# One fixed instruction list kept through the first GEMM half: conversion, stores, steps and the list's order changed together

## The chip, the cores and the metric

The kernel runs on one core of a Trainium2 chip. The metric is the device time in microseconds (us) from launch to the end of the program. Each engine (TensorE = PE, VectorE = DVE, ScalarE = ACT, GpSimd = POOL, SyncE = SP, which issues most of the DMAs) runs its own instructions in the order in which they were placed, and engines wait for each other through semaphores. The order on each engine is fixed when the program is built.

## The reference

Eight batches of Nystrom attention with 32 landmarks per head feed a dense MLP (W_in, squared ReLU, W_out), whose output goes through a top-1 mixture of eight experts.

```
attention, per batch (8 heads, 576 tokens, 64 wide), landmarks = means over 18 tokens:
    A = softmax(q k_lm^T);  Bm = softmax(q_lm k_lm^T);  C = softmax(q_lm k^T)
    Z = Bm^T / (norm1(Bm) * norminf(Bm) + 1e-6);  6 times: Z = 2 Z - Z Bm Z
    out = A Z C v
MLP:      x = relu(x @ w_in)**2 @ w_out          (512 -> 2048 -> 512)
experts:  e = argmax(x @ w_gate); out = gate * sigmoid(x @ w_og)[e] * (relu(x @ w1[e]) @ w2[e])
```

## The kernel before

**GEMM halves.** The MLP is done per batch b and half c of its tokens (288 columns), in `gemm(b)`. Each of the 16 steps f makes `hp` (6 matmuls of the attention factors `ab` and `gb`), squares it into `gh` + `gl` (high and low part: ACT makes `r` and `gh`, DVE makes `g` and `gl`; in half (0, 0) `g` is on DVE, later on ACT), and two steps later `second` adds 12 matmuls into the four `acc` banks, with W_out as `hi` (ACT) and `lo` (DVE). `ab` is the softmaxed A, transposed and split; `gb` is W_in folded into the batch's 64-wide factor (`chunk`: matmuls `two<-wi,wt`, then `split_g` on ACT and DVE), four chunks of four steps each. So the matmuls of step f need `ab`, `gb`, and two steps later `hi` and `lo`.

**Conversion.** W_in and W_out arrive as 64-bit floats in 32 pieces of 512 KB (`raw`). `convert` is a generator: each turn fetches the piece three ahead, scales one piece (`m` by a cast on POOL, ACT or DVE, and `r` on ACT) and adds the two integer halves of the piece before (`bits`, POOL, written to `wf` or `w`). `cv()` in the prologue and `convert_on(f)` in half (0, 0) turn it, `CONV` turns per step f; `split_out(f)` turns it further when W_out piece f isn't there yet. Converted W_in pieces go back to DRAM (`win`) through a list of held stores, which `release(n)` empties.

**Steps of later batches.** The attention of batch b + 1 (`unit`) is a generator too; `point()` takes `RATES[b, c]` steps at each of its places in the GEMM (58 places in half (0, 0), 64 in others), so that the steps run beside the matmuls. Its parts named below: `sums` and `landmarks` (`lm`), `scores_a` and `scores_c` (both `two<-x,lm` on PE), `softmax_b` (many small DVE instructions on `mb`, `bt`, `bc`), `inverse`, `weights` (`wz`, `wt`), `softmax_a` (`aa`: subtract and multiply on POOL, Exp on ACT, sums on DVE), `transposed_a` (`at`). After `gemm`'s last step of a batch, `finish` writes logits (`pl`) and `route` picks experts (`pt`, `pc`).

**The list of tied operations.** While `self.strict` is true, `in_lane` ties every instruction to the one written before it on its engine, so the engine's order is the order of the code. With `strict` False new instructions follow the last tied one but are free among themselves: a scheduler with its own timing estimate chooses their order. With `strict` None nothing is tied.

```
        if self.strict is not None and hasattr(op, "ins"):
            if name in self.lanes:
                self.follow(op, self.lanes[name])
            if self.strict:
                self.lanes[name] = op
```

Before, the tied list covers the prologue and ends with the last line of `first_g`. In `gemm(0)` at c = 1, f = 0, conversion is finished, the held stores are released and `strict` becomes None.

Of the kernel before, what the change touches and what calls it, by code (L numbers as in the profile page):

```python
# [9 lines left out]
F32 = mybir.dt.float32  # L10
# [7 lines left out]
ALU = mybir.AluOpType  # L18
# [5 lines left out]
LM = 32  # L24
# [16 lines left out]
CONV_BUFS = 3  # L41


CONV = 2.0
SUMS_AT = {3: ("k", 0), 5: ("k", 1), 7: ("q", 0)}
OUT_AHEAD = 3
FIRST_G = (6, 10)
# [1 line left out]
URGENT = 2000  # L49
G_FIRST = 2  # L50

RATES = {(0, 0): 0.2, (0, 1): 0.65}
RATE = 0.4

PACE = 20
# [65 lines left out]
class Kernel:  # L121
# [60 lines left out]
    def convert(self, jobs):  # L182

        nc, pool = self.nc, self.cv
        W = CONV_W
        pieces = [(j, c) for j in range(len(jobs)) for c in range(0, 512, W)]
        st, to = {}, {}
        RB = CONV_AHEAD

        tops = [pool.tile([128, W], I32, tag=f"cm{i}", name="m") for i in range(CONV_BUFS)]
        for m in tops:
            nc.gpsimd.memset(m, 0)  # L200

        def fetch(i):

            j, c = pieces[i]
            raw = pool.tile([128, 2 * W], I32, tag="raw", name="raw", bufs=RB)
            self.raws[i] = nc.sync.dma_start(
                out=raw.bitcast(U16)[:, 0:4 * W - 1], in_=jobs[j][0][:, c:c + W].bitcast(U16)[:, 1:4 * W]
            )
            st[i] = raw

        def scale(i):

            raw, m = st[i], tops[i % CONV_BUFS]
            r = pool.tile([128, W], I32, tag="cr", name="r", bufs=CONV_BUFS)
            top = m.bitcast(F16).rearrange("p (n t) -> p n t", t=2)[:, :, 1]
            high = raw.bitcast(BF16).rearrange("p (n t) -> p n t", t=4)[:, :, 2]
            ops = []
            if self.strict and i > 4 and i % 2:
                ops.append(nc.scalar.activation(out=top, in_=high, func=ACTF.Copy))
            elif self.strict or i % 2:  # L220
                ops.append(nc.gpsimd.tensor_copy(out=top, in_=high))
            else:
                ops.append(nc.vector.tensor_copy(out=top, in_=high))
            ops.append(nc.scalar.activation(
                out=r, in_=raw.rearrange("p (n t) -> p n t", t=2)[:, :, 0].bitcast(U32), func=ACTF.Copy,
                scale=2.0 ** -13,
            ))
            if self.last_h is not None:
                for op in ops:
                    self.follow(op, self.last_h)  # L230
            st[i] = m, r

        def bits(i):
            (j, c), (m, r) = pieces[i], st.pop(i)
            if c == 0:
                to[j] = jobs[j][1]()
            self.halves(to[j][:, c:c + W].bitcast(I32), m, r, ALU.add)

        n = len(pieces)
        for i in range(min(RB - 1, n)):  # L240
            fetch(i)
        yield STEP
        per = 512 // W
        for i in range(n + 4):
            if i + RB - 1 < n:
                fetch(i + RB - 1)
            if i < n:
                scale(i)
            if 0 <= i - 1 < n:
                bits(i - 1)  # L250
            if i >= 2 and (i - 2) % per == per - 1 and i - 2 < n:
                j = (i - 2) // per
                jobs[j][2](to.pop(j))
            yield STEP
# [246 lines left out]
    def sums(self, u, nm, hg):  # L501

        if nm + "s" not in u:
            u[nm + "s"] = self.sm.tile([128, 2, 2, D], F32, tag=f"{nm}s", name="sums", bufs=1)
        s, t = u[nm + "s"][:, hg], self.qk[nm, u["b"], hg]
        if not u["pe"]:
            t = t.rearrange("p s d -> p (s d)")
            x = self.sm.tile([128, SEG // 2 * D], F32, tag="st", name="st", bufs=1)
            add = lambda out, in0, in1: self.nc.gpsimd.tensor_tensor(out=out, in0=in0, in1=in1, op=ALU.add)
            n = SEG * D // 4  # L510
            for c in range(0, 2 * n, n):
                self.paced(add(x[:, c:c + n], t[:, c:c + n], t[:, 2 * n + c:3 * n + c]))
            for w in (256, 128, 64):
                add(x[:, 0:w], x[:, 0:w], x[:, w:2 * w])
            twice = [128, 2, D]
            add(s, x[:, 0:D].unsqueeze(1).to_broadcast(twice), x[:, 512:576].unsqueeze(1).to_broadcast(twice))
            return
        for d in range(0, D, D // 2):
            ds = slice(d, d + D // 2)
            total = self.nc.vector.tensor_reduce(  # L520
                out=s[:, 0, ds], in_=t[:, :, ds].rearrange("p s d -> p d s"), axis=AX.X, op=ALU.add
            )
            if self.last_h is not None:
                self.follow(total, self.last_h)
# [102 lines left out]
    def exp_a(self, u, hg):  # L627

        nc = self.nc
        ma = u["ma"][:, :, hg]  # L630
        af = u["aa"][:, hg].rearrange("p (n l) -> p n l", l=LM)
        wide = [128, NB, LM]
        nc.vector.tensor_reduce(out=ma[:, 0], in_=af, axis=AX.X, op=ALU.max)
        yield
        nc.vector.tensor_tensor(
            out=af, in0=af, in1=ma[:, 0].unsqueeze(2).to_broadcast(wide), op=ALU.subtract
        )
        nc.scalar.activation(out=af, in_=af, func=ACTF.Exp, scale=SCALE / SEG)
        yield
        nc.vector.tensor_reduce(out=ma[:, 1], in_=af, axis=AX.X, op=ALU.add)  # L640
        nc.vector.tensor_scalar(out=ma[:, 1], in0=ma[:, 1], scalar1=1e-9, scalar2=None, op0=ALU.add)
        nc.vector.reciprocal(out=ma[:, 2], in_=ma[:, 1])
        yield
        most = ma[:, 2].unsqueeze(2).to_broadcast(wide)
        if hg:
            nc.vector.tensor_tensor(out=af, in0=af, in1=most, op=ALU.mult)
        else:
            self.halves(af, af, most, ALU.mult)
        yield
        self.transposed_a(u, hg)  # L650

# [55 lines left out]
    def softmax_b(self, u):  # L707
# [27 lines left out]
        nc.vector.reciprocal(out=mb[:, :, 3], in_=mb[:, :, 2])  # L735
        nc.vector.tensor_tensor(out=bm, in0=bm, in1=mb[:, :, 3].unsqueeze(2).to_broadcast(wide), op=ALU.mult)
        bt = sm.tile([128, 3, 2, LM], F32, tag="bt", name="bt", bufs=1)
        for hg in range(2):
            nc.vector.transpose(out=bt[:, 0, hg], in_=bc[:, hg, 0:LM])
        nc.vector.tensor_reduce(out=mb[:, :, 4], in_=bm, axis=AX.X, op=ALU.add)  # L740
        nc.vector.tensor_reduce(out=mb[:, :, 5], in_=bt[:, 0], axis=AX.X, op=ALU.add)
        yield STEP
# [11 lines left out]
        nc.vector.tensor_tensor(out=mb[:, :, 8], in0=mb[:, :, 6], in1=mb[:, :, 7], op=ALU.mult)  # L754
        nc.vector.tensor_scalar(out=mb[:, :, 8], in0=mb[:, :, 8], scalar1=1e-6, scalar2=None, op0=ALU.add)
        nc.vector.reciprocal(out=mb[:, :, 9], in_=mb[:, :, 8])
        nc.vector.tensor_scalar(out=mb[:, :, 10], in0=mb[:, :, 9], scalar1=-1.0, scalar2=None, op0=ALU.mult)
        if not u["early"]:
            self.norm_c(u)
            self.diagonal(u, bc)  # L760
        yield STEP
# [98 lines left out]
    def powers(self, u):  # L860
# [4 lines left out]
        for i in range(7):  # L865
# [7 lines left out]
            if i == 0:  # L873
                e = new.tile(pair, F32, tag="ee", name="ee", bufs=2)
                for g in range(2):
                    nc.vector.scalar_tensor_tensor(
                        out=e[:, g], in0=pe[:, g], scalar=mb[:, g, 10:11], in1=self.i32, op0=ALU.mult, op1=ALU.add
                    )
            elif i < 6:
                e = new.tile(pair, F32, tag="ee", name="ee", bufs=2)  # L880
                nc.vector.tensor_copy(out=e, in_=pe)
            if i:
                f = new.tile(pair, F32, tag="ef", name="ef", bufs=2)
                if i == 1:
                    nc.vector.tensor_tensor(
                        out=f, in0=self.i32.unsqueeze(1).to_broadcast(pair), in1=was_e, op=ALU.add
                    )
                else:
                    nc.vector.tensor_tensor(out=f, in0=was_f, in1=pf, op=ALU.add)
# [123 lines left out]
    def prologue(self, right):  # L1013
# [24 lines left out]
            self.transposed(u, "q", 1, i)  # L1038
        cv()
        self.scores_a(u, 0)  # L1040
        cv()
        self.scores_a(u, 1)
        self.landmarks(u, "q")
        cv()
        self.load_v(0, 0)
        self.load_v(0, 1, early)
        sb = self.softmax_b(u)
        next(sb)
        for i in range(2):
            self.scores_c(u, i)  # L1050
        a0, a1 = self.exp_a(u, 0), self.exp_a(u, 1)
        next(a0)
        next(sb)
        next(sb)
        pw = self.powers(u)
        next(pw)
        cv(2)
        self.exp_c(u, 0)
        next(pw)
        cv()  # L1060
        self.exp_c(u, 1)
        next(pw)
        self.transposed_c(u, 0)
        next(a0)
        next(pw)
        cv()
        next(a1)
        next(pw)
        for j in (1, 2):
            self.transposed_c(u, j)  # L1070
        next(a1)
        self.norm_c(u)
        next(pw)
        cv()
        self.values(u, 0)
        for _ in range(2):
            next(a0)
        next(pw)
        next(pw, None)
        self.values(u, 1)  # L1080
        self.first_values(u)
        cv()
        self.last_values(u)
        self.weights(u)
        next(a0, None)
        for _ in range(3):
            next(a1, None)
        cv(2)

    def first_g(self):  # L1090

        self.banks = [self.acc]
        with self.tc.high_priority(URGENT):
# [1 line left out]
            while self.g_done < G_FIRST:  # L1095
                self.first_g_of(self.g_done)
            self.drain()
        self.strict = False
        self.banks = [self.aux]
        for _ in range(3):  # L1100
            self.load_next()
# [81 lines left out]
    def convert_on(self, f):  # L1183

        self.due_conv += CONV
        while self.due_conv >= 1.0:
            self.due_conv -= 1.0
            next(self.conv, None)
        if f > 0:
            self.release(2)  # L1190
        if f in SUMS_AT:
            self.sums(self.ahead, *SUMS_AT[f])

# [535 lines left out]
```

## Time and profile before

| | before |
|---|---|
| median of 3 runs | 1269.85 us (1269.71 to 1271.21) |
| the profiled execution's own time | 1268.21 us |
| its span, first to last instruction | 1266.1 us |
| PE busy in the span | 1218.2 us (96%) |
| DVE, ACT, POOL busy | 609.0, 610.7, 408.8 us |
| mean granted PE clock | 0.98 of full speed |

The span falls into the prologue (0 to 40 us), half (0, 0) (to the first `hp` of half (0, 1) at 105.1 us), half (0, 1) (to the first `hp` of batch 1 at 165.5 us), and fourteen more halves and the experts, in which PE hardly ever waits. A PE matmul's time doubles where the granted clock is 0.5, so busy time there isn't work at full speed.

### The profile page before, as it was taken

The numbers are of one execution on the slowest core, as the hardware profiler recorded it, in microseconds if no ns is written. First come the engines' busy times: TensorE is split into PE (matmuls) and PEld (weight loads), VectorE is DVE, ScalarE is ACT, GpSimd is POOL, SyncE is SP. The second block draws the span as 40 slices with busy tenths as digits, with TensorE's granted clock in tenths as the row PEclk, the third lists the DMA queues.
The fourth block names the chain that finished last, engine by engine and source line by source line (L and its number), as shares of the span: only waits on it lengthen the run. The fifth ranks groups of instructions, "written<-read, shape, count | busy, mean of one in ns | idle before, by whom it ended". The sixth has DMA issues, their size and how long they took to land.

```text
span 1266.1 us, 25177 instructions
## 1 busy us (share of the span) xinstructions
PE 1218.2 (96%) x9858; PEld 1085.4 (86%) x9858; DVE 609.0 (48%) x1524; ACT 610.7 (48%) x1414; POOL 408.8 (32%) x547
## 2 busy tenths in 40 slices
PE   6779979999999999999999999999999999999996
PEld 4569858989989989988988989998888888888885
DVE  8884645645745735745735632233333323323231
ACT  6666435455455465465465454553333433424331
POOL 5872331341341341341251100052342424424220
PEclk8799979999999999999999999999999999999998
DMA  8982234052051151152141210053435444443331
GB/s 297 320 275 105 76 105 143 20 189 71 25 189 58 39 190 54 42 185 65 36 153 57 88 68 20 20 161 86 135 101 155 125 117 150 114 122 111 92 96 39
DMA packets 88408, 142.25 MB, mean 112 GB/s; under 512 B 6430, under 2 KB 61758, under 8 KB 84702
## 3 DMA queue, kind: packets, MB, share of 16 engines
q1 hardware_dynamic: 87854, 139.97, 34.4%
q8 instruction: 80, 1.31, 0.4%
q0 software_dynamic: 288, 0.43, 0.1%
q14 instruction: 42, 0.34, 0.1%
q10 hardware_dynamic: 144, 0.20, 0.0%
HBM read 117.47 MB, written 23.11 MB: 111 GB/s over the span
## 4 chain that ended last, share of the span: by engine, by line
PE 88%; DVE 7%; POOL 2%; issue 1%; ACT 1%; DMA 1%; POOLq 0%; DVEq 0%; ACTq 0%
PE hp L459 31%; PE acc L459 29%; PE y L459 16%; PE two L455 3%; PE bank L455 2%; PE bank L103 1%; PE bank L467 1%; DVE x L554 1%; PE pl L455 1%; DVE lo L103 1%; DMA raw<-in_moe_w_in_dram 1%; PE pt L1331 1%; DVE mb L103 1%; DVE gl L103 0%; DVE ma L657 0%
## 5 line engine op out<-in xcount | busy, mean ns | idle before, releaser
L459 PE MATMUL acc<-gl,hi 128*128 128x288 f32 x964 | 270.0, 297 | 2.1 <-DVE gl L1237 1.5
L459 PE MATMUL acc<-gh,lo 128*128 128x288 f32 x964 | 268.8, 296 | 0.0
L459 PE MATMUL hp<-ab,gb 128*128 128x288 f32 x1434 | 242.3, 304 | 3.4 <-ACT gb L1154 2.7
L1237 DVE TENSOR_TENSOR gl<-g,gh 128x288 fp32r<-128x288 f32 x224 | 114.0, 510 | 238.2 <-ACT g L1236 236.6
L459 PEld LDWEIGHTS hp<-ab,gb 128*128 128x128 f32 x1434 | 203.2, 190 | 25.4 <-issue 12.4
L459 PE MATMUL y<-s,h 128*128 128x512 f32 (+1 forms) x896 | 223.0, 396 | 0.8 <-ACT h L1474 0.5
L459 PEld LDWEIGHTS hp<-xs,s 128*128 128x128 f32 x1536 | 212.2, 188 | 7.5 <-DVE ls L1685 0.3
L459 PE MATMUL hp<-xs,s 128*128 128x288 f32 x1536 | 217.1, 295 | 0.2 <-DVE ls L1685 0.2
L1231 ACT ACTIVATE r<-hp 128x288 f32<-128x288 f32 x224 | 91.9, 410 | 228.5 <-PE hp L459 227.9
L459 PE MATMUL acc<-gh,hi 128*128 128x288 f32 x964 | 200.1, 301 | 0.0
L459 PEld LDWEIGHTS y<-s,h 128*128 128x128 f32 (+1 forms) x896 | 160.6, 184 | 37.7 <-ACT h L1474 0.7
L459 PEld LDWEIGHTS acc<-gl,hi 128*128 128x128 f32 x964 | 181.5, 188 | 7.1 <-DVE gl L1237 2.6
L459 PEld LDWEIGHTS acc<-gh,lo 128*128 128x128 f32 x964 | 181.1, 188 | 1.4 <-issue 1.4
L270 POOL TENSOR_TENSOR s<-r,s 128x256 fp32r<-128x256 f32 x128 | 102.0, 818 | 234.9 <-ACT s L258 234.9
L459 PEld LDWEIGHTS acc<-gh,hi 128*128 128x128 f32 x964 | 150.6, 189 | 18.4 <-ACT gh L1232 12.6
L1474 ACT ACTIVATE h<-hp 128x288 fp32r<-128x288 f32 x128 | 52.5, 411 | 188.1 <-PE hp L459 170.8
L1477 DVE SCALAR_TENSOR_TENSOR h<-hp,h 128x64 fp32r<-128x64 f32 (+2 forms) x192 | 62.6, 354 | 167.2 <-ACT h L1474 166.8
L258 ACT CAST s<-r 128x512 fp32r<-128x512 f32 x128 | 77.5, 617 | 70.3 <-PE y L459 56.0
L1232 ACT ACTIVATE gh<-r 128x288 fp32r<-128x288 f32 x224 | 99.5, 444 | 8.2 <-PE acc L459 1.7
L264 DVE TENSOR_TENSOR s<-r,s 128x512 fp32r<-128x512 f32 x64 | 51.1, 798 | 102.2 <-ACT s L258 102.1
L565 POOL COPY x<-x 32x576 f32<-32x576 f32 x48 | 32.7, 680 | 207.4 <-DVE x L554 100.9
L1236 ACT ACTIVATE g<-r 128x288 f32<-128x288 f32 x224 | 96.0, 429 | 0.5 <-DVE gl L1237 0.5
(263 smaller groups left out, 1362.3 us busy)
## 6 DMA issues: line engine op xcount, KB each, us to landing
r<-in_moe_w_dram SPq DMA_DIRECT2D x128, 256.0 KB
wi<-win SPq DMA_DIRECT2D x28, 1024.0 KB
t<-in_k_dram SPq DMA_DIRECT2D x16, 576.0 KB
t<-in_q_dram SPq DMA_DIRECT2D x16, 576.0 KB
v<-in_v_dram SPq DMA_DIRECT2D x32, 288.0 KB
x_d<-x SPq DMA_DIRECT2D x16, 576.0 KB
xr<-x_d SPq DMA_DIRECT2D x16, 576.0 KB
raw<-in_moe_w_in_dram SPq DMA_DIRECT2D x16, 511.8 KB
```

Source lines behind the costliest of these rows:

```text
L103: return self.kernel.in_lane(self.name, fn(*args, **kw))
L258: hi = self.nc.scalar.copy(out=t[:, 0], in_=raw)
L264: lo_eng.tensor_tensor(out=t[:, 1], in0=raw, in1=t[:, 0].bitcast(F32), op=ALU.subtract)
L270: self.nc.gpsimd.tensor_tensor(out=out[:, p], in0=in0[:, p], in1=in1[:, p], op=op)
L455: self.in_run(lambda: self.nc.tensor.matmul(out, **kw))
L459: mm = self.nc.tensor.matmul(out, **kw)
L1231: nc.scalar.activation(out=r, in_=hp[:, 0:HC], func=ACTF.Relu)
L1232: nc.scalar.activation(out=gh, in_=r, func=ACTF.Square)
L1236: nc.scalar.activation(out=g2, in_=r, func=ACTF.Square)
L1237: nc.vector.tensor_tensor(out=gl, in0=g2, in1=gh.bitcast(F32), op=ALU.subtract)
L1474: nc.scalar.activation(out=h[:, t0:t1], in_=hp[:, 0:HC], func=ACTF.Relu)
L1477: nc.vector.scalar_tensor_tensor(out=h[:, to + a:to + z], in0=hp[:, a - t0:z - t0], scalar=0.0, in1=h[:, a:z].bitcast(F32), op0=ALU.max, o ...
```

## The change

- `strict` stays true until it becomes None at (c = 1, f = 0): all of half (0, 0) is in the order of the code.
- `CONV` 2.0 to 1.5. Three W_in stores are released at the end of the prologue and one per step f from f = 0 (two from f = 1 before).
- In half (0, 0) the casts of even pieces go to POOL and of odd ones to DVE (before the other way round).
- `RATES` of batch 0: 0.2 to 0.25 and 0.65 to 0.7.
- The prologue's list: `landmarks` of q between the two `scores_a`, `scores_c` before the V loads, a different place for most `cv` turns (12 before and now), `transposed_c` earlier, both `softmax_a` chains finished before `values`.
- Smaller edits: the two halves of a q tile are added on POOL before DVE's reduction (batch 0); the second head group's multiply in `exp_a` goes from DVE to POOL; one transpose in `softmax_b` for two; a factor of -1 is folded into the signs that follow (batch 0).

```diff
-CONV = 2.0
+CONV = 1.5
-RATES = {(0, 0): 0.2, (0, 1): 0.65}
+RATES = {(0, 0): 0.25, (0, 1): 0.7}
...
-            if self.strict and i > 4 and i % 2:
+            if i < 5 or i % 2 == 0:
+                ops.append(nc.gpsimd.tensor_copy(out=top, in_=high))
+            elif self.last_h is None:
                 ops.append(nc.scalar.activation(out=top, in_=high, func=ACTF.Copy))
-            elif self.strict or i % 2:
-                ops.append(nc.gpsimd.tensor_copy(out=top, in_=high))
             else:
                 ops.append(nc.vector.tensor_copy(out=top, in_=high))
...
+        if u["early"] and nm == "q":
+            x = u["early"].tile([128, SEG // 2, D], F32, tag="st", name="st", bufs=2)
+            n = SEG // 2
+            self.halves(x, t[:, 0:n], t[:, n:], ALU.add)
+            t = x
...
-        if hg:
-            nc.vector.tensor_tensor(out=af, in0=af, in1=most, op=ALU.mult)
-        else:
-            self.halves(af, af, most, ALU.mult)
+        self.halves(af, af, most, ALU.mult)
...
-        for hg in range(2):
-            nc.vector.transpose(out=bt[:, 0, hg], in_=bc[:, hg, 0:LM])
+        nc.vector.transpose(out=bt[:, 0], in_=bm)
...
+        self.landmarks(u, "q")
+        self.scores_a(u, 1)
         cv()
-        self.scores_a(u, 1)
-        self.landmarks(u, "q")
-        cv()
-        self.load_v(0, 0)
-        self.load_v(0, 1, early)
...
-        cv(2)
+        next(a1, None)
+        cv(3)
+        self.release(3)
...
-        self.strict = False
         self.banks = [self.aux]
...
-        if f > 0:
-            self.release(2)
+        self.release(1)
```

The first place is DVE at the start of half (0, 0). Before, the scheduler's order is this (`lo` is the low part of a W_out piece, `g` and `gl` belong to a step f each, told apart by the number behind `g`, `sums` are batch 1's):

```order
L103 TENSOR_TENSOR g_808<-r 128x288
L103 TENSOR_REDUCE sums<-t 128x32 x2
L103 TENSOR_TENSOR gl<-g_808,gh 128x288
L103 TENSOR_TENSOR g_867<-r 128x288
L103 CAST m<-raw 128x512
L103 TENSOR_TENSOR g_924<-r 128x288
L103 TENSOR_REDUCE sums<-t 128x32 x2
L103 TENSOR_TENSOR lo<-w,hi 128x512 x3
L103 TENSOR_TENSOR gl<-g_867,gh 128x288
```

Now DVE's rows from the split of `gb` on, that is from step f = 0, are:

```order
L103 TENSOR_TENSOR gb<-bank,gb 128x512 x4
L103 TENSOR_TENSOR lo<-w,hi 128x512
L103 TENSOR_TENSOR g_744<-r 128x288
L103 TENSOR_TENSOR gl<-g_744,gh 128x288
L103 CAST m<-raw 128x512
L103 TENSOR_TENSOR lo<-w,hi 128x512
L103 TENSOR_TENSOR g_772<-r 128x288
L103 TENSOR_TENSOR gl<-g_772,gh 128x288
```

The first `lo`, which stood behind the `g` of step f = 4 and came three at a time, now stands ahead of the `g` of f = 0, and each step has one.

The second place is PE between the last step of batch 0 and the first of batch 1. Before (`wz` is batch 1's factor, `two<-wi,wt` its first `gb` chunk, `sums` the landmarks of batch 2, `hp` the first steps of batch 1):

```order
L467 MATMUL bank<-ident,wz 128x128
L455 MATMUL two<-wi,wt 32x512 x8
L467 MATMUL bank<-ident,sums 128x128
L459 MATMUL hp<-ab,gb 128x288 x6
L467 MATMUL bank<-ident,sums 128x128
L459 MATMUL hp<-ab,gb 128x288 x6
```

Now:

```order
L467 MATMUL bank<-ident,wz 128x128
L467 MATMUL bank<-ident,sums 128x128 x4
L455 MATMUL two<-x,lm 32x288 x8
L455 MATMUL bank<-lm 32x32 x8
L455 MATMUL pl<-x_2381,wg 32x288 x4
L455 MATMUL two<-wi,wt 32x512 x8
L1331 MATMUL pt<-sel,lg 128x16 x4
L1331 MATMUL pt<-sel,lg 64x16
L1336 MATMUL pt<-sel,lg 128x16
L459 MATMUL hp<-ab,gb 128x288 x6
```

All four landmark transposes of batch 2, its first `scores_c`, its `softmax_b` product, the logits and the routing of batch 0 have moved ahead of batch 1's first `hp`; before, the transposes stood between its first four and the rest behind them.

The third place is POOL there. Before, between the last multiply of `aa` and the second half of batch 1's `ab`:

```order
L270 TENSOR_TENSOR aa<-aa,ma 128x288 x2
L509 TENSOR_TENSOR st<-st 128x256
L509 TENSOR_TENSOR st<-st 128x128
L509 TENSOR_TENSOR st<-st 128x64
L270 TENSOR_TENSOR ab<-at,ab 128x288 x2
L509 TENSOR_TENSOR sums<-st 128x128
```

Now (`st` and `sums` are the landmark sums of batch 2, four sets of them):

```order
L270 TENSOR_TENSOR aa<-aa,ma 128x288 x2
L509 TENSOR_TENSOR st<-st 128x128
L509 TENSOR_TENSOR st<-st 128x64
L509 TENSOR_TENSOR sums<-st 128x128
L509 TENSOR_TENSOR st<-t 128x288 x2
L270 TENSOR_TENSOR ab<-at,ab 128x288 x2
L509 TENSOR_TENSOR st<-st 128x256
L509 TENSOR_TENSOR st<-st 128x128
L509 TENSOR_TENSOR st<-st 128x64
L509 TENSOR_TENSOR sums<-st 128x128
```

POOL has got one set further when `ab` comes: the third set is whole and the fourth begun, where before the second was not yet written.

## Rows read from the trace of the kernel before

**Rows 1.** Busy time of stretches: PE, PEld, DVE, ACT, POOL, granted clock, DMA.

```profile
0.00:40.00 40.00, 25.27 (x481) 17.28 (x481) 31.90 (x89) 24.42 (x52) 25.77 (x42) 0.80 0.83 273
40.00:105.10 65.10, 53.30 (x392) 44.19 (x393) 57.16 (x96) 43.98 (x97) 48.05 (x57) 0.91 0.81 278
105.10:165.50 60.40, 54.99 (x512) 48.95 (x510) 30.32 (x74) 27.54 (x67) 18.50 (x28) 0.96 0.29 93
165.50:225.00 59.50, 56.34 (x546) 47.81 (x547) 33.62 (x97) 30.17 (x76) 14.03 (x23) 0.90 0.33 119
```

**Rows 2.** Waits of PE in 40 to 105.1: sum, times, longest.

```profile
PE acc L103 <- DVE lo L103: 4.4, 4, 2.0
PE hp L103 <- ACT r L103: 2.9, 5, 1.6
```

**Rows 3.** Groups of DVE in 40 to 105.1: count, busy, mean, idle before them.

```profile
L103 DVE TENSOR_TENSOR lo<-w,hi 128x512 fp32r<-128x512 f32 x16 | 14.0, 873 | 2.3 <-ACT hi L103 1.9
L103 DVE TENSOR_TENSOR g<-r 128x288 f32<-128x288 f32 x16 | 10.4, 647 | 2.0 <-ACT r L103 1.9
...
L915 DVE TENSOR_TENSOR dg<-bc,h 128x256 f32<-128x256 f32 x1 | 1.0, 964 | 0.0
L103 DVE COPY bt<-mb 128x128 f32<-128x128 f32 x1 | 0.7, 747 | 0.0
L103 DVE TENSOR_TENSOR mb<-mb 128x2 f32<-128x2 f32 x1 | 0.7, 678 | 0.0
```

**Rows 4.** DVE in order of time, half (0, 0): start, length, instruction, idle before.

```profile
46.07 0.98 DVE L103 TENSOR_TENSOR g<-r 128x288 f32<-128x288 f32 x1
...
51.30 0.46 DVE L103 TENSOR_TENSOR g<-r 128x288 f32<-128x288 f32 x1
```

**Rows 5.** ACT in order of time, a wait for a converted piece.

```profile
89.55 0.62 ACT L103 CAST hi<-w 128x512 fp32r<-128x512 f32 x1 [3.72 <-POOL w L103]
```

**Rows 6.** The prologue in order of time: DVE, POOL.

```profile
4.75 8.62 DVE L103 TENSOR_REDUCE sums<-t 128x32 f32<-128x576 f32 x8
...
11.89 0.77 POOL L103 CAST m<-raw 128x512 f16<-128x512 bf16 x1 [7.50 <-DMA raw<-in_moe_w_in_dram]
...
32.45 1.30 POOL L103 TENSOR_TENSOR aa<-aa,ma 128x288 f32<-128x288 f32 x2 [1.74 <-DVE ef L103]
```

**Rows 7.** POOL in order of time, end of half (0, 1).

```profile
158.89 1.30 POOL L270 TENSOR_TENSOR aa<-aa,ma 128x288 f32<-128x288 f32 x2 [4.58 <-DVE ma L664]
...
162.15 1.54 POOL L270 TENSOR_TENSOR ab<-at,ab 128x288 fp32r<-128x288 f32 x2 [0.35 <-ACT ab L258]
163.65 0.45 POOL L509 TENSOR_TENSOR sums<-st 128x128 f32<-128x128 f32 x1
164.18 1.54 POOL L509 TENSOR_TENSOR st<-t 128x288 f32<-128x288 f32 x2
165.80 1.66 POOL L509 TENSOR_TENSOR st<-st 128x256 f32<-128x256 f32 x3
```

**Rows 8.** PE in order of time, first to fifth step of batch 1.

```profile
165.55 2.06 PE L459 MATMUL hp<-ab,gb 128*128 128x288 f32 x6 [1.67 <-ACT gb L1154]
...
179.78 1.18 PE L1331 MATMUL pt<-sel,lg 128*128 128x16 f32 x10
...
185.17 2.06 PE L459 MATMUL hp<-ab,gb 128*128 128x288 f32 x6 [1.07 <-ACT gb L1154]
```

**Rows 9.** PE busy and granted clock there, in stretches of 5 us.

```profile
180.00:185.00 5.00, 3.01 (x47) 0.93 0.30 79
185.00:190.00 5.00, 4.83 (x29) 0.50 0.33 132
```

**Rows 10.** DVE in order of time: split of a `gb` chunk, batch 2's `softmax_b`.

```profile
165.53 0.69 DVE L1155 TENSOR_TENSOR gb<-two,gb 128x512 fp32r<-128x512 f32 x1 [0.65 <-ACT gb L1154]
...
184.64 0.21 DVE L724 TENSOR_REDUCE mb<-bank 128x2 f32<-128x64 f32 x1
...
188.07 0.29 DVE L751 TENSOR_REDUCE mb<-bn 128x4 f32<-128x128 f32 x1
```

More of the change, by code (lines that the diff above doesn't have):

```diff
@@ L756, in softmax_b @@
         nc.vector.reciprocal(out=mb[:, :, 9], in_=mb[:, :, 8])
-        nc.vector.tensor_scalar(out=mb[:, :, 10], in0=mb[:, :, 9], scalar1=-1.0, scalar2=None, op0=ALU.mult)
         if not u["early"]:
+            nc.vector.tensor_scalar(out=mb[:, :, 10], in0=mb[:, :, 9], scalar1=-1.0, scalar2=None, op0=ALU.mult)
             self.norm_c(u)
@@ L876, in powers @@
                     nc.vector.scalar_tensor_tensor(
-                        out=e[:, g], in0=pe[:, g], scalar=mb[:, g, 10:11], in1=self.i32, op0=ALU.mult, op1=ALU.add
+                        out=e[:, g], in0=pe[:, g], scalar=mb[:, g, 9:10], in1=self.i32, op0=ALU.mult,
+                        op1=ALU.subtract,
                     )
@@ L885, in powers @@
                     nc.vector.tensor_tensor(
-                        out=f, in0=self.i32.unsqueeze(1).to_broadcast(pair), in1=was_e, op=ALU.add
+                        out=f, in0=self.i32.unsqueeze(1).to_broadcast(pair), in1=was_e, op=ALU.subtract
                     )
@@ L1050, in prologue @@
             self.scores_c(u, i)
+        cv()
+        self.load_v(0, 0)
+        self.load_v(0, 1, early)
         a0, a1 = self.exp_a(u, 0), self.exp_a(u, 1)
@@ L1056, in prologue @@
         next(pw)
-        cv(2)
+        cv(3)
         self.exp_c(u, 0)
         next(pw)
-        cv()
         self.exp_c(u, 1)
@@ L1065, in prologue @@
         next(pw)
+        for j in (1, 2):
+            self.transposed_c(u, j)
+        next(a1)
+        next(pw)
         cv()
@@ L1068, in prologue @@
         next(pw)
-        for j in (1, 2):
-            self.transposed_c(u, j)
-        next(a1)
         self.norm_c(u)
         next(pw)
-        cv()
+        next(pw, None)
+        for _ in range(2):
+            next(a0)
         self.values(u, 0)
         for _ in range(2):
-            next(a0)
-        next(pw)
-        next(pw, None)
+            next(a1)
         self.values(u, 1)
@@ L1085, in prologue @@
         next(a0, None)
-        for _ in range(3):
-            next(a1, None)
-        cv(2)
+        next(a1, None)
+        cv(3)
+        self.release(3)
     def first_g(self):
```

## The prediction, written before the changed kernel ran

> **What bounds the kernel now.** I read the busy time by stretches first. After 225 us nothing can be had, since the change doesn't touch it and PE hardly waits; before, four stretches matter [rows 1]. In the prologue PE is 25.3 of 40 us busy, DVE 31.9. In half (0, 0) PE is busy for 53.3 of 65.1 us, partly at half speed (granted clock 0.91), while DVE is busy for 57.2 us, POOL for 48.1 and ACT for 44.0, and the DMA engines for 0.81 of the time. No engine is the bound alone, but DVE is nearest to it, with 7.9 us of idle time. In half (0, 1) PE is idle for 5.4 us and in the 59.5 us behind it for 3.2, with granted clocks of 0.96 and 0.90.
>
> The view of waits then says for what PE waits in half (0, 0): `lo` on DVE (4.4 us) and `r` on ACT (2.9 us) [rows 2]. The order of the code before says why `lo` is late: the scheduler put the first three of them behind the `g` of step 4, so PE ran five `hp` ahead and had no `acc` to do. In DVE's groups `lo`, `g` and the like take their time twice over: `g` has a mean of 0.65 us [rows 3], and took 0.46 while POOL did nothing, 0.98 while POOL worked [rows 4].
>
> **The change part by part.** The sum goes by the profiled execution, 1268.2 us, which is 1.6 us under the median of the three runs (1269.85).
>
> *Half (0, 0).* The tied list gives each step its `lo`, and it stands ahead of the step's `g`; PE gets `acc` work two steps behind `hp` all the way. I take DVE as the bound. Of its 57.2 us the second part of batch 1's `softmax_b` leaves for half (0, 1), where the new order has it and where DVE is idle for half of the time [rows 1]: `dg` 1.0, `bt` 0.7, `mb` 0.7 [rows 3], 2.4 us, the smaller pieces not counted. The casts only change between odd and even pieces (one more or less, 0.5 us), and steps taken at 0.25 for 0.2 make 14 turns of 58 places where it was 11, all of them in that order already. That leaves 54.8 us. Of the 7.9 us of idle time I keep half, 4.0, because waits of one engine for another remain in any order: 58.8 us for 65.1, **-6.3 us**. Bounds: no idle time is -10.3, all of it -2.4. POOL with its 48.1 us, ACT with 44.0 and PE fit inside 58.8; the DMA engines' 0.81 becomes 0.90, since the same pieces and stores move.
>
> The stores: three of 256 KB now go out ahead of batch 1's tiles and of the next pieces. At the 278 GB/s of this stretch [rows 1] that is 2.8 us for a piece which the list needs only some steps later; the conversion in front of it hides it. If that cover is gone, it is +2.8 once. Fewer conversion turns per step (1.5 for 2) cost nothing by themselves, since `split_out` takes the missing turn when a W_out piece isn't there; what that can cost is the first rival.
>
> At one price the skill and the rows can be laid side by side. In the rows `g` doubles while POOL works [rows 4]. The Trainium skill, GPSIMD Engine Reference, Key points, says that GpSimd shares its SBUF interfaces with VectorE and that instructions with two SBUF inputs contend with it. By that rule the excess stays as long as POOL's work stays, and the sum is as above; if it went with the order, `g` alone would give back 16 times 0.19 us, 3 us more.
>
> *Prologue.* Eight DVE reductions take 8.62 us, 1.08 each, in one row with no gap [rows 6]; four of them now read half as many elements. Estimated at half the time that is 2.1 us less on DVE, but POOL must add the halves first. POOL is free then: it waits 7.5 us for its first piece [rows 6]. I take **-1.0**, between 0 and -2.1. The multiply that goes from DVE to POOL (like the one there, 1.30 us [rows 6]) stands in front of the conversion of W_in's last needed pieces; if nothing hides it, it costs +1.3. The sign, the one transpose for two and the earlier `landmarks` are a few tenths on DVE, inside the same bounds.
>
> *Between batch 0 and 1.* The order has changed here, and not for the good of the first `hp`. Before: POOL ends the last `aa` multiply at 160.2, starts `ab` at 162.15 [rows 7], and `hp` starts at 165.55, waiting for the split of `gb` [rows 8], 5.4 us after `aa`. Now POOL does the rest of the third set of sums (two of the three adds that take 1.66 together, about 1.1, and 0.45) and the first adds of the fourth (1.54) before `ab`: 3.1 us, then `ab` 1.54, then the fourth set's rest (1.66 and 0.45) [rows 7]: 6.7 us after `aa`. Only then come batch 2's last `landmarks`, `scores_c` and `softmax_b`, since PE has `scores_c` ahead of the `gb` chunk, and DVE has `softmax_b` ahead of the chunk's split. DVE's part of `softmax_b` took from 184.64 to 188.4, 3.7 us [rows 10]; for the transposes, the copy and `scores_c` I put 2.5 us (nothing, if POOL is early, to 5); the split is two turns of 0.69 with 0.65 between [rows 10], of which `hp` has to wait for about 2.0. That makes 14.9 us for 5.4: 9.5 us later.
>
> Behind it a second wait ends. Before, `hp` of the fifth step came at 185.17, after another wait [rows 8], with 2.0 us idle between 180 and 185 and 4.8 us of matmuls at clock 0.50 in the next five, 2.4 us lost [rows 9]. The clock falls after a stretch in which PE had little to do; one stretch instead of two loses it once. And `pt` (1.18) [rows 8], with `scores_c`, the logits and the small product (1.6 together, estimated from their sizes beside `pt` and `hp`), is done inside the first wait. That gives 7.2 us back. Net **+2.3**, between -3 (POOL early) and +9.5 (nothing given back).
>
> Sum: -6.3 - 1.0 + 2.3 = -5.0; 1268.2 - 5.0 + 1.6 = **1264.8, say 1265 us**.
>
> **The rivals.**
>
> *The list waits (slower).* In the tied list ACT has `hi` of step f ahead of that step's `r`, and DVE `lo` ahead of `g`. If a converted W_out piece is late, the `hp` of the next step can't start, for `r` hasn't emptied its bank. Before, the scheduler let `r` pass. The trace has such a wait: ACT stood for 3.72 us on POOL's `w` [rows 5]. With 12 turns in the prologue and 1.5 per step, W_out pieces 5, 7 and 9 are not there when `split_out` asks for them, and it has to take a turn; three waits of 3.7 are 11.2 us: -5.0 + 11.2 = +6.2, 1276. It decides from the second such wait on. Against it: two steps of `acc` lie between a `lo` and its use, some 5 us. The Trainium skill, TensorE: Matmul & The Clock Gate, Architectural detail, says that ScalarE's and VectorE's queues are strictly first in, first out, so that nothing passes a waiting instruction; that rule speaks for this rival, and the rows agree as far as they go (nothing on ACT ran in those 3.72 us).
>
> *The gain is eaten.* Either the DMA engines, at 0.90, hold the half at its old length (-1.0 + 2.3 = +1.3, 1271), or the second wait between the batches stays beside the longer first one (-7.3 + 9.5 = +2.2, 1272). For the first speaks that POOL waited for pieces in the prologue; against it, that PE's own waits in the half go back to DVE and ACT [rows 2]. I put the case at 1271.
>
> *More than that.* DVE loses all its idle time (-10.3) and the wait between batches costs nothing more: -11.3, 1258.5.
>
> **How the numbers follow.** The forecast gets 0.46 (1260 to 1269), the waiting list 0.18, the eaten gain 0.18, the larger gain 0.18. The range that leaves out about one in ten on each side is 1256 to 1275. About 0.2%, 2.5 us, is what a measurement of this kernel can tell from no change, so that faster is below 1267.3 and slower above 1272.4: from the forecast 0.42 and the larger gain 0.18 come 0.61 faster with a little of the eaten gain; the waiting list and a third of the eaten gain make 0.24 slower; 0.15 remain.
>
> **What would show it.** In the profile after: the first `hp` of half (0, 1) at 97 to 99 us in place of 105; PE's wait for `lo` in that half under 2 us; DVE busy for 53 to 56 us in it. Between the batches one long PE gap in place of two, `hp` of batch 1 some 15 us after POOL's last `aa`, and the stretch behind it without a second fall of the clock. The prediction is wrong if ACT shows waits of 3 us for `w` in the half, if raw pieces are waited for there, or if the gap between the batches is longer than 20 us.

## The result and the profile after

| | before | after |
|---|---|---|
| median | 1270.17 us (1269.71 to 1271.21, 4 runs) | 1285.12 us (1283.3 to 1286.83, 4 runs) |
| ratio, 95% interval | 1 | 1.0116 [1.0099, 1.0134] |
| profiled execution, its span | 1268.21, 1266.1 us | 1285.73, 1283.7 us |

The change makes the kernel 15 us slower; the forecast was 1265. The stretches after (columns as in [rows 1]; the first `hp` of half (0, 0) is at 41.13, of half (0, 1) at 117.61, of batch 1 at 193.50 us):

```profile
0.00:41.00 41.00, 26.27 (x481) 17.66 (x481) 28.65 (x86) 24.83 (x53) 28.50 (x46) 0.75 0.81 255
41.13:117.61 76.48, 54.50 (x381) 47.22 (x382) 57.21 (x83) 44.95 (x97) 51.63 (x62) 0.82 0.75 259
117.60:175.00 57.40, 53.91 (x506) 49.89 (x504) 30.07 (x82) 25.75 (x63) 13.95 (x21) 1.00 0.23 73
175.00:193.50 18.50, 8.76 (x72) 4.35 (x73) 6.68 (x24) 4.17 (x11) 7.42 (x13) 0.55 0.16 50
```

Half (0, 0) has become 76.5 us long. DVE has as much to do in it as before (57.2 us, 57.16 in [rows 1]), but stands idle for 19.3 us in place of 7.9. Waits of PE in 41 to 117.6 us (against [rows 2]), and DVE's groups there (against [rows 3]):

```profile
PE hp L103 <- ACT r L103: 14.0, 5, 5.5
PE two L103 <- POOL wf L103: 6.8, 2, 4.0
```

```profile
L103 DVE TENSOR_TENSOR lo<-w,hi 128x512 fp32r<-128x512 f32 x16 | 13.9, 866 | 10.9 <-ACT hi L103 10.9
L103 DVE TENSOR_TENSOR g<-r 128x288 f32<-128x288 f32 x16 | 11.6, 724 | 2.0 <-ACT r L103 2.0
...
L103 DVE TENSOR_REDUCE sums<-t 128x32 f32<-128x576 f32 x8 | 9.0, 1173 | 0.0
L103 DVE CAST m<-raw 128x512 f16<-128x512 bf16 x11 | 8.3, 757 | 0.0
```

PE's wait for `lo` (4.4 us before) is gone, as predicted; waits for `r` and for converted pieces of W_in have taken its place. DVE waits 10.9 us at `lo` for `hi`, with casts and reductions behind it in its list. Two places in order of time, on ACT, DVE and PE, and what POOL waits for behind the first (start, length, instruction, idle before):

```profile
45.93 0.62 ACT L103 CAST hi<-w 128x512 fp32r<-128x512 f32 x1 [3.88 <-DMA win<-wf]
...
73.42 0.58 ACT L103 CAST gb<-two 128x512 fp32r<-128x512 f32 x1 [5.29 <-DVE gb L103]
```

```profile
46.58 0.69 DVE L103 TENSOR_TENSOR lo<-w,hi 128x512 fp32r<-128x512 f32 x1 [3.09 <-ACT hi L103]
...
48.12 0.46 DVE L103 CAST m<-raw 128x512 f16<-128x512 bf16 x1
...
68.50 4.29 DVE L103 TENSOR_REDUCE sums<-t 128x32 f32<-128x576 f32 x4
72.71 0.68 DVE L103 TENSOR_TENSOR gb<-two,gb 128x512 fp32r<-128x512 f32 x1
```

```profile
48.73 1.92 POOL L103 TENSOR_TENSOR wf<-m,r 128x256 int32<-128x256 int32 x2 [4.41 <-DVE m L103]
```

```profile
66.27 1.06 PE L103 MATMUL hp<-ab,gb 128*128 128x288 f32 x6
...
74.89 1.81 PE L103 MATMUL hp<-ab,gb 128*128 128x288 f32 x6 [5.45 <-ACT r L103]
```

At 41 us, `hi` of step 0 waits 3.88 us for a *store*: it is written into the buffer of W_in piece 0 (tag `wa0`), which `win` must have read first. The prediction did not see that. DVE waits with it, and POOL waits 4.41 us for the cast `m` that stands behind `lo` on DVE. At 68 us four reductions stand ahead of the split of `gb`; ACT waits 5.29 us for it, and PE 5.45 us for the `r` behind it. Six `hp` matmuls took 1.06 us before that and 1.81 right after it (granted clock 0.71 in 75 to 80 us, 0.82 in the half, 0.91 before [rows 1]).

Between the batches, POOL and PE (against [rows 7, 8]):

```profile
175.55 1.30 POOL L270 TENSOR_TENSOR aa<-aa,ma 128x288 f32<-128x288 f32 x2 [6.05 <-DVE ma L666]
...
179.76 1.54 POOL L270 TENSOR_TENSOR ab<-at,ab 128x288 fp32r<-128x288 f32 x2
181.25 1.65 POOL L509 TENSOR_TENSOR st<-st 128x256 f32<-128x256 f32 x3
182.98 0.45 POOL L509 TENSOR_TENSOR sums<-st 128x128 f32<-128x128 f32 x1
```

```profile
178.24 0.47 PE L467 MATMUL bank<-ident,sums 128*128 128x128 f32 x1 [2.88 <-POOL sums L509]
183.49 0.48 PE L467 MATMUL bank<-ident,sums 128*128 128x128 f32 x1 [3.84 <-POOL sums L509]
...
193.50 1.79 PE L459 MATMUL hp<-ab,gb 128*128 128x288 f32 x6
```

`hp` comes 16.65 us after the end of `aa` (176.85); predicted were 14.9. There is one stretch of waits there in place of two, at a granted clock of 0.55; the clock is 0.62 in the 5 us behind it and 1.00 in the six stretches of 5 us after that (against [rows 9]). Of the 17.6 us by which the span grew, 12.5 have arisen at the first `hp` of half (0, 1) (117.6 for 105.1) and 28 at that of batch 1; 21 are left eight steps later, 17.6 at the end.

### The profile page after: what moved, and what is told of

Its sections match the earlier page's. It is cut to its first block, busy times and chain, and to the rows that moved or that the text cites. A ratio compares the mean times of both kernels' runs of the same rounds, so it can differ in the third digit from the quotient of the medians.

```text
span 1283.7 us, 25167 instructions
## 1 busy us (share of the span) xinstructions
PE 1218.6 (95%) x9858; PEld 1088.1 (85%) x9858; DVE 601.5 (47%) x1515; ACT 611.8 (48%) x1414; POOL 412.5 (32%) x552
## 4 chain that ended last, share of the span: by engine, by line
PE 86%; DVE 6%; DMA 3%; POOL 2%; ACT 2%; issue 1%; SPq 0%; POOLq 0%; DVEq 0%; ACTq 0%
PE hp L459 30%; PE acc L459 28%; PE y L459 16%; PE two L455 3%; PE bank L455 2%; DVE x L559 1%; PE bank L103 1%; PE bank L467 1%; DMA win<-wf 1%; PE pl L455 1%; PE pt L1331 1%; DMA raw<-in_moe_w_out_dram 1%; POOL wf L103 1%; DVE ma L659 1%; POOL w L103 1%
## 5 line engine op out<-in xcount | busy, mean ns | idle before, releaser
L459 PE MATMUL hp<-ab,gb 128*128 128x288 f32 x1434 | 239.5, 302 | 1.2 <-ACT gb L1155 0.6
L1237 DVE TENSOR_TENSOR gl<-g,gh 128x288 fp32r<-128x288 f32 x224 | 110.2, 493 | 247.6 <-ACT g L1236 246.6
L459 PEld LDWEIGHTS hp<-ab,gb 128*128 128x128 f32 x1434 | 202.0, 189 | 15.6 <-issue 7.0
L459 PE MATMUL acc<-gh,hi 128*128 128x288 f32 x964 | 197.5, 300 | 0.0
L459 PEld LDWEIGHTS acc<-gh,hi 128*128 128x128 f32 x964 | 148.9, 188 | 24.4 <-ACT gh L1232 19.3
```

What stands on the lines that cost most here:

```text
L459: mm = self.nc.tensor.matmul(out, **kw)
L1237: nc.vector.tensor_tensor(out=gl, in0=g2, in1=gh.bitcast(F32), op=ALU.subtract)
```

## The experiments

All ran beside the kernel before on their chip. Ratios have 95% intervals; us between kernels are differences of ratios times 1270. Such a difference carries the intervals of both runs: some 3 us either way against the changed kernel, some 2 us between two untied runs. "Half" is by how much the first `r` of half (0, 1) comes later than before in the profiled execution (106.69), "batch 1" the same of its ninth `r` (201.47).

| run | median us | ratio | half | batch 1 |
|---|---|---|---|---|
| changed kernel | 1285.1 | 1.0116 [1.0099, 1.0134] | +11.9 | +21.0 |
| e1_untied | 1275.8 | 1.0032 [1.0021, 1.0043] | +5.5 | +12.0 |
| e2_conv2 | 1284.7 | 1.0097 [1.0079, 1.0115] | +11.5 | +21.0 |
| e3_hi1 | 1283.2 | 1.0089 [1.0067, 1.0111] | +9.5 | +18.7 |
| e4_rates | 1288.4 | 1.0119 [1.0097, 1.0142] | +12.5 | +20.4 |
| e5_tie_before | 1283.8 | 1.0093 [1.0065, 1.0121] | +7.6 | +15.6 |
| e6_untied_rates | 1274.5 | 1.0031 [1.0020, 1.0042] | +4.8 | +4.6 |
| e7_three | 1283.4 | 1.0097 [1.0073, 1.0120] | +10.9 | +20.4 |
| e8_untied_hi1 | 1275.1 | 1.0038 [1.0027, 1.0049] | +4.5 | +11.1 |
| e9_free_act | 1285.5 | 1.0111 [1.0093, 1.0128] | +13.1 | +22.2 |
| e10_free_pe | 1281.1 | 1.0087 [1.0067, 1.0107] | +9.7 | +16.0 |
| e11_free_dve | 1278.5 | 1.0059 [1.0042, 1.0077] | +6.1 | +14.2 |
| e12_free_pool | 1281.3 | 1.0081 [1.0064, 1.0098] | +10.6 | +18.9 |
| e13_free_m | 1282.8 | 1.0089 [1.0072, 1.0106] | +10.0 | +18.1 |
| e14_free_sums | 1281.4 | 1.0074 [1.0057, 1.0091] | +12.0 | +20.4 |
| e15_prologue | 1267.9 | 0.9984 [0.9973, 0.9995] | +1.3 | -1.9 |
| e16_rates_before | 1272.6 | 1.0020 [1.0008, 1.0031] | +2.6 | +8.1 |
| e17_releases | 1272.5 | 1.0018 [1.0009, 1.0027] | +2.6 | +3.4 |
| e18_conv15 | 1271.3 | 1.0005 [0.9995, 1.0014] | +7.5 | +3.9 |

**Which part costs.** The tie is the rule that fixes the order of half (0, 0) to that of the code. e1 ends the tie where it ended before, e4 restores the rates, e6 does both:

```diff
@@ first_g: e1, e6
             self.drain()
+        self.strict = False
@@ e4, e6
-RATES = {(0, 0): 0.25, (0, 1): 0.7}
+RATES = {(0, 0): 0.2, (0, 1): 0.65}
```

> The changed kernel, but the tie ends where it ended before, after the first two pieces of G, so that the scheduler again sets the order of half (0, 0). CONV, the prologue's list and the rates stay. If the tied list is what makes the half longer (ACT stands at hi and at the split of gb with r queued behind it), the first hp of half (0, 1) comes at 105 to 109 us instead of 117.6 and the time falls by 9 to 12 us, to 1273 to 1276. If the half is longer for the late conversion (CONV 1.5) or for the longer prologue, the time stays within 3 us of 1285. The long gap between batch 0 and 1 (20 us from the last acc to hp) stays by either.

> The changed kernel with the old rates, 0.2 and 0.65, so that between batch 0 and 1 PE has the first W_in chunk and hp ahead of the scores and the logits of the next steps, as before. If the later start of hp there (some 10 us, of which some 4 come back later) is the second cost beside the half, the time falls by 4 to 10 us, to 1275 to 1281, and the first hp of batch 1 stands within 8 us of the last aa of POOL. If that work is only moved and returns behind, as the prediction's net of +2.3 has it, the time falls by 0 to 3 us.

> The changed kernel without the tie and with the old rates 0.2 and 0.65. Against the run without the tie alone (1275.8) it tells what the junction between batch 0 and 1 costs net. If the late hp there is paid back, as the prediction has it (+2.3 net), the time falls by 0 to 4 us, to 1272 to 1276; if it is not, by 5 to 9 us, to 1267 to 1271. If the new rates gain (as the run with the old rates in the tied kernel, 3 us slower, says), it rises to 1277 to 1280.

The tie costs 10.7 us (e1). The new rates cost nothing that can be measured without the tie (e6 against e1), and with it the old ones gain nothing (e4): they put `hp` ahead again, but batch 1 is no sooner (+20.4). So in this kernel no second loss is seen in the long gap between the batches. Of e4's two readings the first (4 to 10 us) is out, and the second, work only moved, is left at its lower end.

**Is it the tie, or the tie with this list?** e5 ties the list of the kernel before:

```diff
@@ kernel before, first_g
-        self.strict = False
@@ prologue, last line
+        self.release(3)
@@ convert_on
-        if f > 0:
-            self.release(2)
+        self.release(1)
```

(The conversion's casts stay on the engines where they were.)

> The kernel before with the tie alone carried on through half (0, 0), and with the stores of W_in released as in the changed kernel (three at the end of the prologue, then one per step), since hi would otherwise wait for a store that stands behind it. CONV 2.0, the old prologue list and the old rates stay. If the tie costs by itself (each engine's waits stop the whole step), the half becomes 7 to 12 us longer and the time is 1277 to 1284. If the tie is only bad with the changed list (late conversion, three store waits), it costs 0 to 4 us: 1270 to 1275.

e5 is 11.8 us slower than the kernel before. The releases cost 4.3 in another pair of runs, untied and with the new prologue (below); if they cost as much here, an estimated 7.5 is left for the tie. So the list of the kernel before loses too. DVE's wait at `lo` in its half (0, 0):

```profile
DVE lo L103 <- ACT hi L103: 3.5, 4, 1.5
```

That is 3.5 us for the 10.9 of the changed kernel, so a tied list can lose without a long wait there.

**Single waits.** e2 takes the late conversion away, e3 the wait for the store, e7 does both and moves the reductions so that no four stand in a row ahead of the split of `gb`; e8 is e3 without the tie.

```diff
@@ e2, e7
-CONV = 1.5
+CONV = 2.0
@@ split_out: e3, e7, e8
-hi = self.wop.tile([128, 512], F32R, tag=f"wa{f}", name="hi")
+hi = self.wop.tile([128, 512], F32R, tag=f"wx{f}" if f < 1 else f"wa{f - 1}", name="hi")
@@ e7
-SUMS_AT = {3: ("k", 0), 5: ("k", 1), 7: ("q", 0)}
+SUMS_AT = {2: ("k", 0), 4: ("k", 1), 7: ("q", 0)}
```

> The changed kernel with CONV = 2.0 for 1.5. If the two waits of PE for converted W_in pieces (2.8 and 4.0 us) and ACT's waits for raw W_out pieces lie on the path, the half becomes 5 to 8 us shorter: 1277 to 1280. If they only lie beside ACT's other waits, or if more conversion per step makes POOL and the DMA engines the bound instead, the time stays within 3 us of 1285, and other waits (hi for a store, r for POOL) grow.

> The changed kernel, but hi of step 0 has a buffer of its own and hi of step f is put where W_in piece f - 1 was, not f, so each store of a W_in piece has one step more before hi needs its place. If the waits of hi for the store (3.9, 1.3 and 2.6 us on ACT) are what delays r and hp, 5 to 8 us are gained: 1277 to 1280, and ACT shows less than 1 us of such waits. If r would be late anyway (the half is bound by late conversion or by the split of gb), the time stays within 2 us of 1285 although those waits are gone.

> The changed kernel, tied, with three of its waits removed at once: hi one buffer ahead of the stores, CONV 2.0, and the sums of k of batch 1 at steps 2 and 4 for 3 and 5, so that not four reductions stand ahead of the split of gb at step 6. If the loss is a sum of single waits, it is 7 to 12 us faster: 1273 to 1278. If each wait that goes only makes room for the next (late raw pieces, POOL's conversion, the order itself), it stays above 1280.

> The changed kernel without the tie, with hi one buffer ahead of the stores. In the run without the tie, the first r of half (0, 0) is 4 us later than before, behind a hi that waits 3.3 us for the store of the first W_in piece. If that wait is on the path, the time falls by 3 to 5 us, to 1271 to 1273; if the half ends when the conversion ends anyway, it stays at 1275 to 1277.

None gains as much as the waits that it removes: the intervals of e2, e3 and e7 touch that of the changed kernel, and e8 gains nothing over e1. ACT's longest waits in half (0, 0) of e7:

```profile
ACT r L103 <- DMA raw<-in_moe_w_out_dram: 14.1, 7, 5.9
ACT gb L103 <- DVE gb L103: 5.0, 2, 4.3
```

The waits for stores (7.8 us on ACT in the changed kernel) are gone, and those for raw pieces have grown from 3.5 to 14.1. The wait for `gb` hardly changed (6.0 to 5.0), so e7 did not remove the third one: a reduction of q, itself waiting for its tile, stands ahead of the split there. In this list a wait that is removed makes room for the next.

**Whose order.** e9 to e12 take one engine out of the tie of half (0, 0); e13 and e14 only DVE's casts `m`, or its reductions `sums`:

```diff
@@ in_lane; free is set at the end of first_g: ("scalar",), ("tensor",), ("vector",) or ("gpsimd",)
-            if self.strict:
+            if self.strict and name not in self.free:
                 self.lanes[name] = op
@@ e13, scale
-                ops.append(nc.vector.tensor_copy(out=top, in_=high))
+                ops.append(self.tc.nc.vector.tensor_copy(out=top, in_=high))
@@ e14, sums
-            total = self.nc.vector.tensor_reduce(
+            total = (self.nc if self.last_h is None else self.tc.nc).vector.tensor_reduce(
```

> The changed kernel with the tie of half (0, 0) taken off ACT alone; PE, DVE, POOL and the stores on SP stay in the list's order. If ACT's order is what costs (hi, the conversion's r and the unit's copies in front of the GEMM's r, for which PE's hp waits 14 us), most of the 9.5 us that the run without any tie gained comes back: 1276 to 1279. If the engines hold each other whichever one is tied, it gains less than 3 us: above 1282.

> As the run with ACT free, but PE free alone. If PE's own order costs (transposes, scores and the chunk of G stand ahead of hp and wait for data), 5 to 9 us come back: 1276 to 1280. If PE only waits for ACT's r, freeing it changes less than 3 us: 1282 to 1287.

> As the run with ACT free, but DVE free alone. By the prediction's rival (lo ahead of g, the reductions ahead of the split of gb) 4 to 8 us come back: 1277 to 1281. If DVE's waits (10.9 us for hi) only follow ACT's, under 3 us: 1282 to 1287.

> As the run with ACT free, but POOL free alone. POOL does nearly nothing but the conversion in the half, in the order in which the pieces come, so I expect no more than 2 us by either theory: 1283 to 1287. A gain of 4 us or more would say that the order of POOL's adds among the casts is what holds the conversion.

> The changed kernel, tied, but the conversion's casts m on DVE stand outside the tie. If the loss is the ring lo waits for hi, hi for a converted piece, the piece for m, and m stands behind lo, this run gains nearly what DVE free as a whole gained (7 us): 1278 to 1281, and POOL's waits for m (8 us and more in the tied runs) fall under 2. If the casts were not what counted, 1283 to 1286.

> The changed kernel, tied, but batch 1's reductions (sums) on DVE stand outside the tie. If it is the row of four reductions ahead of the split of gb that counts (PE waits 5.5 us behind it), 3 to 6 us come back: 1279 to 1282. If the casts are what counts, under 2 us: 1283 to 1286.

Freeing ACT gains nothing, although `hi`, `r` and `gb` stand there and PE waits for `r`. PE's waits in its half (0, 0):

```profile
PE two L103 <- POOL wf L103: 8.5, 2, 4.9
PE two L103 <- DVE gb L103: 5.8, 1, 5.8
PE hp L103 <- ACT r L103: 5.0, 3, 4.2
```

The wait for `r` fell from 14.0 to 5.0 us, and `gb` on DVE took its place. Freeing PE gains 3.7 us (its interval touches that of the changed kernel), POOL 4.4, more than the 2 expected, so that the order of POOL's adds and casts counts too. Freeing DVE gains most, 7.2 us. These gains add up to 15.9 us, more than the 10.7 of the tie, so they are not separate shares of it; SP, whose DMA issues are tied as well, was not freed alone. The half of that run, and what DVE waits for in it:

```profile
41.23:111.80 70.57, 55.14 (x382) 45.55 (x383) 60.91 (x89) 44.95 (x97) 53.18 (x62) 0.83 0.81 281
```

```profile
DVE lo L103 <- ACT hi L103: 4.2, 4, 1.8
```

DVE is busy for 60.9 of 70.6 us, idle for 9.7 in place of 19.3. Its instructions at the same two places:

```profile
43.53 0.53 DVE L103 CAST m<-raw 128x512 f16<-128x512 bf16 x1
45.84 0.69 DVE L103 TENSOR_TENSOR lo<-w,hi 128x512 fp32r<-128x512 f32 x1 [1.77 <-ACT hi L103]
46.44 0.45 DVE L103 TENSOR_TENSOR g<-r 128x288 f32<-128x288 f32 x1
...
68.21 2.27 DVE L103 TENSOR_REDUCE sums<-t 128x32 f32<-128x576 f32 x2
70.39 0.68 DVE L103 TENSOR_TENSOR gb<-two,gb 128x512 fp32r<-128x512 f32 x1
```

The scheduler still puts `lo` ahead of `g`, in all 16 steps. What it moves are casts, reductions and small steps of batch 1: a cast runs ahead of the first `lo`, and two reductions stand ahead of the split of `gb` in place of four. With e13 3.4 us come back, with e14 5.3. e13's interval touches that of the changed kernel. e14's half is not shorter in its profile, but the profiled execution took 1284.7 us, 3.4 above the median of its four. Which of the two it is stays open.

**The rest.** Without the tie and at the old rates, 4 us of loss remain (e6). e15 takes back the conversion rate and the releases too, so that only the new prologue, the changed casts and the small edits stay; e17 and e18 add one each. e16 is the kernel before with the new rates.

```diff
@@ e15, e17: CONV = 2.0; e18: CONV = 1.5; all without the tie, with the old rates
@@ e15, e18
-        self.release(3)
...
-        self.release(1)
+        if f > 0:
+            self.release(2)
```

> The changed kernel without the tie, with the old rates, CONV 2.0 and the old releases of the stores: of the change only the new list of the prologue is left, with q's sums by POOL's halves, the changed casts and the small edits. The prediction had -1.0 for it (0 to -2.1): 1269 to 1270. If the DMA engines' idle stretch at 35 to 40 us, in which this list moves some 0.7 MB less than the old one, is what makes the half 4.6 us longer, 1272 to 1275.

> The kernel before with the new rates 0.25 and 0.7 alone. The prediction has +2.3 for what they do between batch 0 and 1 (first +9.5, then 7.2 given back): 1272 to 1273. The pair of runs without the tie says +1 to +2. If the late hp isn't paid back: 1277 to 1280; if steps done sooner are a gain by themselves: below 1269.

> The run with the new prologue alone (1267.9), and the new releases beside it: three stores of W_in at the end of the prologue, then one per step. CONV stays at 2.0. If the stores in front of the k tiles and of the raw pieces cost (PE waited 6.6 us for a k tile, hi 3.1 us for a store), most of the 6.6 us come here: 1271 to 1275. If it is CONV, within 1.5 us of 1268.

> The run with the new prologue alone, and CONV = 1.5 beside it, with the old releases. If the slower conversion costs (PE waited 3.8 us for a converted W_in piece at a chunk of G), 1271 to 1275; if the releases do, within 1.5 us of 1268.

With these alone the kernel is 2.0 us *faster* than before; it is the one version that beats both kernels. On top of it the early releases cost 4.3 us and CONV 1.5 costs 2.7 (together 6.0 in e6). SP's queue in e17 and in e15, then PE behind it in e17 and in e15:

```profile
38.01 1.97 SPq L103 DMA_DIRECT2D win<-wf  x3
40.10 1.20 SPq L103 DMA_DIRECT2D raw<-in_moe_w_out_dram  x1
41.34 0.65 SPq L103 DMA_DIRECT2D win<-wf  x1
42.09 0.92 SPq L103 DMA_DIRECT2D t<-in_k_dram  x2
```

```profile
39.92 0.86 SPq L103 DMA_DIRECT2D t<-in_k_dram  x2
```

```profile
48.98 0.87 PE L103 MATMUL bank<-ident,t 128*128 128x128 f32 x3 [6.34 <-DMA t<-in_k_dram]
```

```profile
45.84 0.87 PE L103 MATMUL bank<-ident,t 128*128 128x128 f32 x3 [1.49 <-DMA t<-in_k_dram]
```

Batch 1's k tiles are issued behind four stores and PE has their transposes ahead of `hp`, so it waits 6.3 us for 1.5. `hi` also waits there for a store (3.3 us on ACT), but in e8, where that wait is gone, PE still waits 7.3 us for the tile. With CONV 1.5 (e18) PE waits for `hi` and `lo` instead:

```profile
PE acc L103 <- ACT hi L103: 4.1, 1, 4.1
PE acc L103 <- DVE lo L103: 3.9, 4, 1.9
```

## Why the prediction was wrong

By the runs the change is -2.0 (the prologue's list, the casts and the small edits) + 6.0 (releases and CONV) + 0.1 (rates) + 10.7 (tie) = +14.8 us; measured were 14.7 (0.0116 times 1270). The four are the steps from one run to the next (e15, e6, e1, the changed kernel), so they add up by construction; in another order the prices differ (the rates cost 2.5 in e16, the tie an estimated 7.5 in e5).

**Half (0, 0), -6.3: the step that failed.** It was "Of the 7.9 us of idle time I keep half, 4.0, because waits of one engine for another remain in any order". DVE's work was near (54.8 predicted, 57.2 measured; `g` took 0.72 us for 0.65, so its excess did not go with the order), the idle time was 19.3 us: 76.5 us for 58.8. No row stood behind that half. The order decides how much of a wait can be filled. The cure that the prediction named, `lo` ahead of `g`, did what it should: PE no longer waits for `lo`, and e11, which keeps that order, is faster than the changed kernel. What loses is that all else on DVE has a fixed place too: while `lo` waits for `hi`, a cast that POOL needs stands behind it (e11 gives 7.2 of the 10.7 us back). How much is due to the casts and how much to the reductions is not shown. The Trainium skill, TensorE: Matmul & The Clock Gate, Architectural detail, says that VectorE's and ScalarE's queues are strictly first in, first out; the trace agrees, since nothing ran on DVE in the 3.09 us before `lo`, where e11 has a cast at 43.53. It holds for both kernels: what differs is what was put in front.

**The waiting list (the rival)** had the sign and the rule, but not the size and the place. It counted three waits of `hi` for `w`; those are 1.1 us here, and of the signs that the prediction named, the wait for raw pieces showed (3.5 us on ACT). It missed that `hi` waits for stores, and freeing ACT alone, on which it was built, gained nothing (e9). Nor did the DMA engines hold the half, as the eaten gain had it: their share in it is 0.75 for 0.81.

**Stores, "the conversion in front hides it".** Wrong: 4.3 us (e17 against e15). The k tiles stood behind them, which the prediction did not price, and raw pieces were late too (ACT waits 4.1 us for them in e17, 0.5 in e15). The k tiles were issued 2.2 us later than in e15 (42.09 for 39.92), because SP issued the stores first, and PE could use the first 3.1 us later (48.98 for 45.84), so about 1 us was lost behind the issue. The Trainium skill, DMA: Bandwidth & Descriptors, Queues, rings and completion order, says that each DMA engine takes the descriptors of a queue's ring in order. The trace agrees as far as that 1 us goes.

**CONV, "cost nothing by themselves".** 2.7 us without the tie (e18 against e15). In the tied list it can't be told from nothing (e2).

**Prologue, -1.0.** The number is inside its bounds, by luck: -2.0, interval -3.4 to -0.6 (e15), which holds the changed casts and the small edits too. The prologue itself hardly became shorter: the first `hp` of half (0, 0) comes at 40.16 in e15 and at 40.32 before, and at 41.13 in the changed kernel. In e15 the first `hp` of half (0, 1) is even 1.8 us later (106.89 for 105.13), and that of batch 1 is 2.2 us sooner (163.30 for 165.55): the gain arises in half (0, 1), for which the prediction had no such term, and its cause stays open. DVE's reductions on half as many elements took 0.62 us each in the changed kernel, a little over the half that was estimated (against 1.08 in [rows 6]):

```profile
10.11 1.23 DVE L103 TENSOR_REDUCE sums<-st 128x32 f32<-128x288 f32 x2 [1.04 <-POOL st L103]
```

**Between the batches, +2.3.** The net is met only in the kernel before, where the rates cost 2.5 us, interval 1.0 to 3.9 (e16). In the changed kernel no cost is seen (0.1 without the tie, none with it), and the net of e16 is luck, since both of its terms were too small: there `hp` of batch 1 came at 181.58 for 165.55, 16.0 later, of which 2.6 are from the half, so 13.4 for 9.5; at the ninth step 5.5 of these are left (8.1 - 2.6). The two waits of PE for `sums` (5.76 and 2.47 us there) are its main part:

```profile
167.68 0.48 PE L467 MATMUL bank<-ident,sums 128*128 128x128 f32 x1 [5.76 <-POOL sums L509]
...
171.56 0.48 PE L467 MATMUL bank<-ident,sums 128*128 128x128 f32 x1 [2.47 <-POOL sums L509]
```

Where the rest comes back later was not looked into.

## What to carry to other kernels

A fixed order over engines that feed each other lets a late arrival stop all that is written behind it on its engine; a sum of busy times bounds such a stretch only from below. Before tying an order, ask for each instruction that may wait what stands behind it on its engine, and count the buffers that it must find free among its inputs. A single wait taken away tells little there: free one engine at a time to find whose order costs, and look at what then moved. And check where a gain arises, not only its size.

## What the runs showed that was not expected

The engine that shows the waits was not the one whose order cost: PE waited 14.0 us for ACT, and freeing ACT gained 0.6 us (0.5 thousandths, inside the interval), freeing DVE 7.2. And the early releases, which in e17 put four 256 KB stores ahead of two 576 KB tiles, cost 4.3 us; four stores take an estimated 3.8 us at the 278 GB/s of the stretch [rows 1]. Of the 3.1 us by which the tiles came later, 2.2 arose before their transfer, while SP issued the stores.
